# A new order by hand for the steady part of a fused attention and maxout kernel: 151 visits, searched on

## The chip, the cores and the metric

The kernel runs on one core of a Trainium2 chip. A core has a matrix engine (TensorE, PE in the profile), two engines that can read the matrix engine's result memory PSUM (ScalarE, ACT; VectorE, DVE), a general engine (GpSimd, POOL) and a queue processor (SyncE, SP) that mostly issues DMAs. PSUM has eight banks here, each 128 rows of 512 float32. The metric is device time in microseconds (us) of one execution; lower is better.

## The reference

Two parts follow each other. First an induced-set attention over x of shape (4, 12544, 128) with 32 inducing vectors, then a maxout layer over all 50,176 rows:

```python
def mab(q, kv):
    s = scale * (q @ kv.transpose(0, 2, 1))
    s = s - s.max(-1, keepdims=True)
    a = np.exp(s)
    a /= a.sum(-1, keepdims=True) + 1e-09
    return a @ kv
h = mab(I, x)          # 32 summary rows for each of the 4 batches
y = mab(x, h)          # each row of x attends to the 32 summary rows
h1 = y @ w1            # 128 -> 1024
h2 = y @ w2
out = np.maximum(h1, h2) @ w_out   # 1024 -> 128
```

## The kernel before

**The algebra.** max(h1, h2) is written as h1 + relu(h2 - h1). Since y is a mix of 32 rows of h, both parts are products of the 32 unnormalized exponentials of a row with small matrices made once per batch: `hwd` (32 x 1024, for h2 - h1) and `m1` (32 x 128, for h1 through w_out). Dividing by the sum of exponentials is left to the end, one factor per row.

**The tiling.** The 98 tiles of 128 rows in each batch are grouped in blocks. A block has four row groups q = 0 to 3, one for each quarter (32 rows) of the matrix engine's array, with up to four tiles in each; shapes are listed in `shapes`. There are 28 blocks, 0 to 27, seven to a batch, and 108 groups (a block's q with its tiles).

**The pieces of work in the steady part.** Each is a word of a list.

- `s` stages a block: scores of its tiles (L655) and their exponentials by ScalarE (L665).
- `p` is a visit: the array is used as four row quarters, and each pick names a quarter, a PSUM bank and who empties it. A pick makes one bank of h2 - h1 (L964). Then `relu_out` moves it to memory through a relu, on ScalarE (pick ends in `a`, L910) or VectorE (`v`, L908). A pick with `+` is emptied together with the next one as a double piece of 1024 columns. Endings `l`, `k`, `L` add the `m1` products of a group. Several `p` words without other work of TensorE between them make one visit; there are 151 visits.
- `d` with a count makes that many products of relu tiles with w_out (L843) into the open group's bank; `o` opens a group in a bank. When a group has all its products, `evict_group` multiplies it with the reciprocals and stores it: on VectorE (L878), or on ScalarE (L885) where the string `EVICT` has a 1; the store is a DMA on SP's queue (L893), from one of six buffers.
- The reciprocals of a block's sums come in one of two ways. `g` has SP transpose the exponentials by DMA (L699), and POOL adds them up and raises them to the power -1 (L708, L712). `n` makes the sums with TensorE (L727, four columns for each tile) and VectorE takes the reciprocal (L736); `n` with a plus does two blocks.
- `x`, `c`, `r`, `t`, `a`, `e`, `h`, `w`, `m` prepare the next batch: DMA transposes of x on SP (L230), scores and exponentials (L391, L403), DMA transposes of these on SP (L421), the accumulation of h (L436, L466/L468), and the small matrices (L475, L510, L561, L569).

**What sets the order.** `PLAN` is a list of such words, written out by hand from a search, and `play` issues their instructions in that order on every engine. Each engine and each queue runs its own instructions in order; semaphores hold an instruction until its data and its buffer are there. So the list fixes the order of TensorE's work, the order in which each evicting engine takes its banks, and the order of DMAs on SP's queue.

```python
if vector:
    nc.vector.tensor_scalar(out=dst, in0=src, scalar1=0.0, scalar2=None, op0=ALU.max)
else:
    nc.scalar.activation(out=dst, in_=src, func=AF.Relu)
...
for word in PLAN.split():
    play(word)
```

The first 22 us (loads, transposes and the first batch's summary) are issued ahead of the list and have an order of their own, `HEAD`.

Of the kernel before, what the change touches and what calls it, by code (L numbers as in the profile page):

```python
# [144 lines left out]
def kernel(  # L145
# [114 lines left out]
    with tc.manual_schedule(engines={ET.PE, ET.DVE, ET.Activation, ET.Pool, ET.SP}):  # L260
# [612 lines left out]
        def evict_group(g):  # L873
            osb = osbs[:, evicted[0] % NOUT, :, :]
            evicted[0] += 1
            q, n, blk = g.q, g.n, g.blk
            if EVICT[groups.index(g)] == "0":
                nc.vector.tensor_mul(  # L878
# [136 lines left out]
        p02a24a33vl:0000213 d17 p05v17a20a31v s2 g3 s3 o4 d17 p06+17a35vl p00+11a32v:021 d15 o3 d6 x1.6 x1.7  # L1015
        p07v15+26a32v d18 p04a17a20+31v p02a15+26al:0023100 d8 o4 d11 p17v20v31al d13 p12+33a p05+26v c1.0.7 s1
        d8 o0 d7 p02+13v25+36a x1.8 d9 p07v14a31a d13 p02v23a35vl p16a34a p07a d3 o1 d22 g4 p06a12+33vl p05v
        p14a c1.1.0 s7 d10 o6 d12 p04a12v23al p10v25v37a x1.9 d17 p04a11+22a33v x1.10 t1.1 g6 d3 o0 d21
        p17v25a34vl p01a12+23a36v:1203 d11 o5 d18 p07v21a34vl p26v p12a33a d12 p00+21a37v c1.2.2 c1.3.4 t1.3 g5
        d2 o3 d12 p00+11v26a37a d19 p02v15al p04v10+21a36a:3012 d1 o7 d19 p05a12v24al d13 o0 d12 p11a p03v26v32a  # L1020
        p17v24+35al:1023000 d20 o1 d9 p23v32al p06a27v p14a35v:10 d8 r1.0 d14 p06v12+23a37v c1.4.4 c1.5.0 a1.1.5
        a1.3.6 p32a t1.5 p03a17v d1 o5 d22 p04a16+37vl p00+11a22v33a d10 o4 d25 p06+17a20vl a1.5.1 p12a p03v25v
        d2 p00+11a26+37a d3 e1.2 d2 o3 d15 h1.5 d5 p10+21a32vl p06a14+25a37v:120310 d12 o2 d10 w1.0.0.0 d2 s1 s7
        s6 p05v10a23+34v d12 w1.1.1.1 d8 o6 d7 p27v35aLl p00a13a24a31v d9 o5 d18 s2 p10v37vl p01a16a23+34a d14
        o2 d7 m1.0 p06+27a31vl d9 o5 d10 p00v13v24vl p01+12a26a37a d18 x2.0 d4 o3 d7 p02a10+21a36a p04vl:100 g8
        x2.1 x2.2 d9 o7 d9 g9 d3 p15v p02a24a33a p00a11vl:2100 d4 o6 d16 n2 d5 p04+15a31a p17v23a32vl:2013000
        d11 o0 d10 x2.3 p27a34v p05a22v31al:0100023 d14 p23a p06v17v34a d8 o5 d6 p11+32a p06v23a x2.4 d20 x2.5
        p14a27v30v p01+12a36al:1203000 d6 o3 d14 p14a p07v x2.6 x2.7 p00+11a22vl:0000321 d10 p05+16v24a37a d7
        x2.8 x2.9 d1 o2 d14 p00a11v24v35a p16+27al d18 o3 d11 p05a10+21v34v p06a27a32al:1023000 d21
        p00a15+26v31v s7 c2.0.4 o2 d19 p03a30vl g10 p06+17a24v35a:1032 d13 o1 d11 x2.10 p03a p10v26v37a d7  # L1030
        p02a14+25vl c2.1.3 s0 c2.2.7 t2.1 g11 d14 o6 d11 p14a22+33vl p05a10a27v31a:1203 d21 p04+15a22+33v c2.3.0
        o7 d23 p21a p05+36vl p00v13+24a32a:2031 d9 o1 d20 p15a36vl p03v14a20a32a:0132 d12 o7 d10 p04v15+26a33v
        d18 p00v p11a g12 p22a p04+15a26vl:0000123 d4 o3 d18 p00+11v22a36v d10 r2.7 s4 c2.4.5 c2.5.2 a2.1.7
        p20+31v p14a25a36al:0100023 t2.3 d4 o7 d22 p02a14v20a31v p05+26a33al:1023000 t2.5 d10 o2 d19 p34v
        p00+11a p07a15a36vl:0000312 g13 d13 o3 d15 p00+11v24a p06al:00001 p17a p22a d17 o5 d5 p04v16a20+31a
        a2.3.7 a2.5.3 p02a14v26v37a d8 p13v20a31al d13 p24v p02a17a36a e2.0 d6 o3 d17 p01+12a24v37v
        p05+26a30al:1023000 d15 o4 d14 p11v32v p07a p05+16a33al:0000231 d15 h2.0 d3 o1 d10 p02v10a26+37v
        p05a13a24al:1012031201202 d12 w2.0.0.0 w2.1.2.1 d10 p05v13v26a37a s4 s0 s2 m2.1 o6 d21 p07v25a34a
        p13v21a30al:1023000 d11 o2 d8 o5 d5 p27a34vLl s3 p06v11+22a30v d14 p37v p04a13a26v d13 p02a10+21a34v o7
        d8 o6 d7 p03v22a35aL d12 p00+21a34v x3.0 p02+13a37vl:1023000 d13 o5 d15 p04a10+21vl g15 p02a16+27a33a  # L1040
        d17 o4 d12 p12v20al p31a p05a16v27a:120 d4 n3 d16 o0 d2 p06a11+22v33a x3.1 d21 p35a p06+27a34vl:0120003
        p01v12+23a:201 x3.2 g16 d9 o5 d16 x3.3 x3.4 p04v16a27a31v g17 x3.5 d16 o0 d5 p02a13v34aL
        p01v16+27al:1203000 d23 p02v13a24+35a d4 o1 d21 x3.6 p06v17a23a32v p14+25a30vl d11 o7 d20 p02+13a26v30v
# [61 lines left out]
```

## Time and profile before

| what | value |
| --- | --- |
| median of three runs | 311.86 us (311.69 to 312.07) |
| the profiled execution, its own time | 311.63 us |
| its span, first to last instruction | 309.9 us |
| mean granted TensorE clock | 0.999 of full speed |
| TensorE busy | 303.4 us |
| ScalarE, VectorE busy | 272.6 us, 271.8 us |
| POOL busy | 128.6 us |
| DMA | 55.55 MB, 179 GB/s on the mean |

Busy times are of the profiled execution and are shares of its span. A matrix product's row in the timeline has its start and a modelled end, and products are pipelined, so the distance between two starts says more than the length of one. "Idle before" in a group row is time in which the engine waited ahead of those instructions, and the arrow names what ended most of it.

### The profile page before, as it was taken

The numbers are of one execution on the slowest core, as the hardware profiler recorded it, in microseconds if no ns is written. First come the engines' busy times: TensorE is split into PE (matmuls) and PEld (weight loads), VectorE is DVE, ScalarE is ACT, GpSimd is POOL, SyncE is SP. The second block draws the span as 40 slices with busy tenths as digits, with TensorE's granted clock in tenths as the row PEclk, the third lists the DMA queues.
The fourth block names the chain that finished last, engine by engine and source line by source line (L and its number), as shares of the span: only waits on it lengthen the run. The fifth ranks groups of instructions, "written<-read, shape, count | busy, mean of one in ns | idle before, by whom it ended". The sixth has DMA issues, their size and how long they took to land.

```text
span 309.9 us, 12504 instructions
## 1 busy us (share of the span) xinstructions
PE 303.4 (98%) x5304; PEld 239.0 (77%) x5304; DVE 271.8 (88%) x443; ACT 272.6 (88%) x478; POOL 128.6 (42%) x194
## 2 busy tenths in 40 slices
PE   7899999999999999999999999999999999999996
PEld 3786777777878787778887887687878877788885
DVE  3369999999888999998899889998899899998995
ACT  3579999998899999899999999989899899988782
POOL 7473003466420084089700187019408916085200
PEclk9999999999999999999999999999999999999999
DMA  7999999995499999999699989994534323333223
GB/s 204 208 227 212 216 227 230 217 197 179 112 223 245 215 222 179 246 239 209 128 246 249 222 172 211 199 229 147 143 93 131 122 78 112 121 122 113 104 98 127
DMA packets 81528, 55.55 MB, mean 179 GB/s; under 512 B 62880, under 2 KB 66496, under 8 KB 81472
## 3 DMA queue, kind: packets, MB, share of 16 engines
q1 hardware_dynamic: 75168, 41.25, 57.1%
q0 software_dynamic: 6160, 13.44, 22.8%
q8 instruction: 41, 0.67, 0.9%
q14 instruction: 15, 0.12, 0.1%
q10 hardware_dynamic: 144, 0.07, 0.1%
HBM read 27.28 MB, written 25.69 MB: 171 GB/s over the span
## 4 chain that ended last, share of the span: by engine, by line
PE 93%; DMA 2%; DVE 2%; issue 1%; ACT 1%; POOL 1%; POOLq 0%; DVEq 0%
PE psall L843 61%; PE psall L964 23%; DMA xn<-in_x_dram 2%; PE psall L655 2%; PE psall L391 2%; PE psall L436 1%; PE psall L298 1%; DVE relus L908 1%; PE psall L360 1%; PE psall L314 1%; ACT xT L305 1%; PE psall L561 0%; POOL xn L222 0%; PE psall L475 0%; DVE osbs L878 0%
## 5 line engine op out<-in xcount | busy, mean ns | idle before, releaser
L910 ACT ACTIVATE relus<-psall 128x512 f16<-128x512 f32 (+1 forms) x371 | 233.7, 718 | 21.7 <-PE psall L964 20.4
L908 DVE TENSOR_SCALAR relus<-psall 128x512 f16<-128x512 f32 (+1 forms) x267 | 194.1, 770 | 18.6 <-PE psall L964 17.1
L843 PE MATMUL psall<-woutp,relus 128*128 128x128 f16 x3104 | 201.1, 219 | 0.0
L843 PEld LDWEIGHTS <-relus 128*128 128x128 f16 x3104 | 174.7, 98 | 31.2 <-issue 26.4
L964 PE MATMUL psall<-e,hwd 32*128 32x512 f16 (+2 forms) x840 | 80.0, 361 | 0.1
L708 POOL TENSOR_TENSOR half<-ed 128x256 f32<-128x256 f16 (+2 forms) x23 | 14.1, 615 | 139.1 <-DMA ed<-e 139.1
L712 POOL TENSOR_TENSOR rd<-den,minus 128x16 f32<-128x16 f32 (+2 forms) x23 | 60.7, 2641 | 1.8
L878 DVE TENSOR_TENSOR osbs<-psall,rd 128x512 f32<-128x512 f32 (+1 forms) x86 | 54.5, 636 | 2.1 <-PE psall L859 0.7
L964 PEld LDWEIGHTS <-hwd 32*128 32x128 f16 x880 | 27.3, 91 | 14.8 <-issue 2.2
L964 PE MATMUL psall<-m,e 32*128 32x128 f16 x376 | 36.6, 216 | 0.0
L964 PEld LDWEIGHTS <-e 32*128 32x128 f16 x376 | 22.5, 92 | 6.3 <-issue 0.5
L708 POOL TENSOR_TENSOR half<-half 128x64 f32<-128x64 f32 (+3 forms) x69 | 22.4, 325 | 5.4
L222 POOL DMA_DIRECT2D xn<-in_x_dram x34 | 18.7, 560 | 5.4 <-DMA xn<-in_x_dram 4.2
L878 DVE TENSOR_TENSOR osbs<-psall,rp 128x512 f32<-128x512 f32 (+3 forms) x20 | 12.8, 642 | 0.9 <-ACT relus L910 0.5
L302 DVE COPY xT<-psall 128x512 f16<-128x512 f16 (+3 forms) x12 | 5.8, 486 | 7.9 <-PE psall L298 7.2
L665 ACT ACTIVATE e<-psall 128x512 f16<-128x512 f32 (+2 forms) x21 | 11.2, 588 | 0.1
L403 ACT ACTIVATE eu<-psall 128x512 f16<-128x512 f32 x18 | 10.9, 610 | 0.0
L305 ACT COPY xT<-psall 128x768 f16<-128x768 f16 (+3 forms) x10 | 5.7, 577 | 4.3 <-PE psall L298 4.2
L298 PE MATMUL psall<-identity,xn 128*128 128x128 f16 x98 | 7.8, 220 | 1.3 <-DMA xn<-in_x_dram 1.1
L655 PE MATMUL psall<-xT,hT 128*32 128x512 f16 (+3 forms) x110 | 8.4, 360 | 0.0
L298 PEld LDWEIGHTS <-xn 128*128 128x128 f16 x98 | 5.6, 98 | 2.9 <-DVE xn L757 1.0
L391 PE MATMUL psall<-xT,inducingT 128*32 128x512 f16 x72 | 6.6, 385 | 0.0
(121 smaller groups left out, 124.5 us busy)
## 6 DMA issues: line engine op xcount, KB each, us to landing
out_dram<-osbs SPq DMA_DIRECT2D x90, 256.0 KB, 2.7
xn<-in_x_dram POOLq DMA_DIRECT2D x23, 448.0 KB, 10.9
out_dram<-osbs SPq DMA_DIRECT2D x10, 128.0 KB, 3.2
xn<-in_x_dram POOLq DMA_DIRECT2D x3, 224.0 KB, 8.9
xT<-xn SPq DMA_TRANSPOSE x33, 4.5
relus<-in_x_dram SPq DMA_DIRECT2D x1, 512.0 KB, 3.7
relus<-in_moe_w_dram POOLq DMA_DIRECT2D x2, 256.0 KB, 5.7
relus<-in_x_dram SPq DMA_DIRECT2D x1, 384.0 KB, 4.2
```

Source lines behind the costliest of these rows:

```text
L222: nc.gpsimd.dma_start(out=xn_at[b, i][p0:p1, 0:n, :], in_=xr[b, p0:p1, k0 : k0 + n, :])
L298: nc.tensor.transpose(ps[:, j, :], xn[:, g + j, :], identity16)
L391: nc.tensor.matmul(out=ps[32 * g : 32 * (g + 1), :], lhsT=inducingT, rhs=xT_tiles[b % 2][:, U * u + 4 * g : U * u + 4 * (g + 1), :], start ...
L655: nc.tensor.matmul(out=ps[32 * q : 32 * (q + 1), 128 * t : 128 * (t + n)], lhsT=hq, rhs=xT[:, c : c + n, :], start=True, stop=True, tile_p ...
L665: nc.scalar.activation(out=blk.e2[:, 0 : 128 * wd], in_=ps[:, 0 : 128 * wd], func=AF.Exp, scale=st[0]["rs"] if blk.b == 0 else scale,)
L708: nc.gpsimd.tensor_tensor(out=dst, in0=cur[:, :, 0:n], in1=cur[:, :, n : 2 * n], op=ALU.add)
L712: nc.gpsimd.tensor_tensor(out=rp[:, 0:wd, :].rearrange("p t q -> p (t q)"), in0=den[:, 0 : 4 * wd], in1=minus1[:, 0 : 4 * wd], op=ALU.pow,)
L843: nc.tensor.matmul(out=g.ps[:, 128 * t : 128 * (t + 1)], lhsT=home[:, 128 * (jb * w4 + t) : 128 * (jb * w4 + t + 1)], rhs=woutp[:, jb, :], ...
L878: nc.vector.tensor_mul(osb[:, 0:n, :], g.ps[:, 0 : n * C].rearrange("p (s c) -> p s c", s=n), blk.rp[:, 0:n, q : q + 1].broadcast_to((128, ...
L908: nc.vector.tensor_scalar(out=dst, in0=src, scalar1=0.0, scalar2=None, op0=ALU.max)
L910: nc.scalar.activation(out=dst, in_=src, func=AF.Relu)
L964: nc.tensor.matmul(**seq.pop(0))
```

## The change

The word list `PLAN` is replaced by another, and the string `EVICT` has no 1 any more. The new list was searched on from there while transfer times were drawn at random and ScalarE and VectorE were stopped at random moments. It plays the same kinds of words for the same blocks and groups with the same 151 visits. What differs is which bank and which engine a pick takes, how the picks of a visit are ordered and paired, where products are split, where the transposes on SP stand, and for which blocks the reciprocals are made by `n` instead of `g`: `n` now serves blocks 0, 1 and 2, 5 and 6, 7 and 8, and 14; before, 0, 1 and 2, 7, and 14. Nothing else in the kernel changes.

```diff
@@ -1008,65 +1008,64 @@
         PLAN = """
-        s6 s5 V0.0.0 H1.0.0 V1.7.1 p02+13v24a p06v10a:110000 p15a p11v27a:1010 W4.0 o0.1 d4.1 d4.1 p22v33a
-        p05a26a m0.7 o4 d4 n1 d8 p23v32aLl:23012122 p07v25a31a:021111 d4 o6 d10 x1.0 p13+24a32v p35a p37v
-        p01a30vl:00012 d14 x1.1 p04a12+23a37v o5 d14 x1.2 p06v10+21a34v d9 x1.3 p07a12v23al d9 p06v10a21a34a
-        x1.4 x1.5 o7 d16 n2+ d1 p03v p15a20a p16v21vl d13 p22a p14a p03v35a d2 o6 d15 p00a31v
...
-        x2.1 x2.2 d9 o7 d9 g9 d3 p15v p02a24a33a p00a11vl:2100 d4 o6 d16 n2 d5 p04+15a31a p17v23a32vl:2013000
...
-        d17 o4 d12 p12v20al p31a p05a16v27a:120 d4 n3 d16 o0 d2 p06a11+22v33a x3.1 d21 p35a p06+27a34vl:0120003
...
-        p06v10+21a37a:1203 o3 d22 p02v24+35a p10+21a36vl:1023000 d10 o7 d3 g25 d7 p02v14v25a36a d14 g27 p23a
...
-        o0 d19 p06+17a33v g26 p01+12a35vl:0000123 d13 o4 d15 p03a16v27al p05a10a21+32v d17 o3 d13 p05v16+27a31v
-        p12a20al d19 o5 d13 p04a16+27v31v p02+23a30al:10230100 d19 o4 d11 p26a p12+33v p17v20+31al:0021321 d5 o5
-        d17 p12+33a p06v10a31vl:010230023 d15 o7 d7 p06a23+34a p01+22v30vl:0012323 d9 o5 d22 p06a11a22vl
-        p07a10a23+34v:0312312 d10 o6 d16 o2 d7 p01a17a23+34v p00aLl:20101 d9 o5 d16 p01v17v23v34a p10a26al d16
-        o1 d24 o2 d16 o1 d8
-        EVICT = "000000000000000000000000000000000000000000000000000000000000000000000000000000000000000000000000000010010000"
+        s6 s5 V0.0.0 H1.0.0 V1.7.1 p02+13v p04v16a20a:21210000 p15a21a p17v W6.0 o0.1 d4.1 d4.1 p22v33a p05a24a
+        m0.1 o6 d4 n7 d8 p23v32aLl:23012122 p01a25v37a:021111 d4 o4 d10 p02+13a36v x1.0 p31a p35v p07a30vl:00012
+        d14 x1.1 p06a12+23a35v o1 d12 p00v16+27a34v d12 p05a12v23al d6 p06+27a x1.2 x1.3 p10a34v x1.4 d2 o5 d16
+        n2+ d1 p23v p14al p16+27v31a:210 d12 p12a p00a24a33v d3 o1 d14 p26a p07v32vl p00a33a d14 p06a14+25v37a
+        s0 s2 d4 o3 d17 p36v p04+15a p00+11a37vl:0000312 x1.5 g3 g4 d15 o2 d5 x1.6 x1.7 p06a14v25v37a d2 x1.8
...
+        p04a11+22vl d8 p03a15a26+37a e1.4 d4 o1 d16 h1.2 n3+ d4 p04+15a20v32v p13a26+37al d12 o0 d7 w1.0.4.0 d5
...
+        g9 p01vl:100 x2.0 d7 o0 d15 x2.1 x2.2 x2.3 x2.4 p05v13v21+32a p06a17al:1200 d1 o4 d13 g10 d3 n5+ d6
...
+        p00+11a36a p25a d16 o2 d13 p23+34v p00+31a p16+27al d3 n5 d16 p03a10+21v34a x3.5 o5 d23 p36a p02+13a27v
...
+        p14v26+37al:0000123 d12 o5 d10 p03v14a21+32a g26 d10 p20v p36a p07a23+34vl:0100023 d12 o1 d15
...
+        p02a15+26a34v:1230 d11 o0 d19 g25 p02+13a27v p34v p05+26a31vl:1023000 d13 o7 d22 p02+13a34v
...
+        p07v16a23+34v p01+22a30al:10230100 d16 o6 d16 p27v p11+32a p13a24v30aL:0021321 o5 d22 p06+17v31a
+        p02a13a34al:001230023 g27 d10 o0 d14 p21v32v p03a26+37al:0102323 d2 o5 d20 p04a11a23vl p02v10v26+37a d12
+        o4 d16 o3 d5 p01+22v30a p06a17aLl:3201013 d11 o5 d15 p06a12a20+31a p14v27al d17 o3 d24 o6 d16 o4 d8
+        EVICT = "000000000000000000000000000000000000000000000000000000000000000000000000000000000000000000000000000000000000"
```

More of the change, by code (lines that the diff above doesn't have):

```diff
@@ L1016 @@
[L1016 to L1025, printed above, removed]
@@ L1031 @@
[L1031 to L1040, printed above, removed]
@@ new lines @@
+        d17 p03a20+31v p14a p06+17a25al:1020300 d8 o3 d11 p14v20v31al d13 p02v16+27a34v s5 c1.0.1 d8 o0 d8
+        p02v14v26+37a d7 p25v p03a31al d16 p32v p04a16+27a33a p15v d1 o1 d21 p04a12vl p05+16v37a:201 s0 c1.1.3
+        d11 o4 d11 p02v p17a20a p05v16a23vl:0000123 x1.9 d17 p07a10v21+32a d4 o5 d20 p03v10v26+37a p11v22a34al
+        d12 o3 d18 p26a p07v20v32al:0130002 p11v34a d13 p05+26a37v c1.2.2 x1.10 c1.3.0 t1.1 t1.3 d1 o4 d11
+        p01a15+26v37a d20 p02v13a30vl p01a p15a26a d1 o7 d21 p03a12v21al d11 o0 d11 p25a34v p16al
@@ new lines @@
+        p03+14a27v30a d2 o6 d17 h3.5 p02+13a27v34v d12 w3.0.1.1 p00v15a37vl s2 s3 s4 d3 o1 d14 p10a25vl g22 g21
+        p07v16a22+33a d18 o4 d11 p00v15+26v37a p12+23a31al d21 o7 d4 w3.1.0.1 p05a12+23v36a:1203 d19
+        p01a14v20v35v p02a23a36al d9 o1 d21 p03+14a p02a30vl:020202021 p15v26a d11 o7 d5 p00v13+34al m3.5 d3 o2
+        d18 p00+11a26vl p04+15v27a33a d14 o6 d8 o0 d17 p04+15a21v37v p12+23aLl:1230111 d15 o1 d17 p04a15v27a36a
+        p02v23a30al:1023000 d15 o4 d15 p25v p06+37a p01+12a33vl:2013000 d17 o0 d3 p07a13a25+36v d20
```

56 lines of the change are left out of this document (32 added, 24 removed).

## The prediction

> **What bounds the kernel now.** I read the page from the top: busy shares, granted clock, then the chain that ended last. After these I took the timeline of TensorE alone, because a busy TensorE in this profile is not yet a TensorE without waits. The page:
>
> ```profile
> span 309.9 us, 12504 instructions
> PE 303.4 (98%) x5304; PEld 239.0 (77%) x5304; DVE 271.8 (88%) x443; ACT 272.6 (88%) x478; POOL 128.6 (42%) x194
> PEclk9999999999999999999999999999999999999999
> PE 93%; DMA 2%; DVE 2%; issue 1%; ACT 1%; POOL 1%; POOLq 0%; DVEq 0%
> PE psall L843 61%; PE psall L964 23%; DMA xn<-in_x_dram 2%; PE psall L655 2%; PE psall L391 2%; PE psall L436 1%; PE psall L298 1%; DVE relus L908 1%; PE psall L360 1%; PE psall L314 1%; ACT xT L305 1%; PE psall L561 0%; POOL xn L222 0%; PE psall L475 0%; DVE osbs L878 0%
> ```
>
> The reader is to see that TensorE holds 93% of the chain, 84 of it in two lines: the products with the output weights (L843) and the visits (L964). The clock is full throughout. The DMA share, 2%, is the first load, which the change does not touch.
>
> Now the prices of TensorE's two kinds of work, from the timeline of TensorE (start, length, line, count):
>
> ```profile
> 257.16 0.73 PE L843 MATMUL psall<-woutp,relus 128*128 128x128 f16 x10
> 257.82 0.40 PE L964 MATMUL psall<-e,hwd 32*128 32x512 f16 x4
> 258.15 1.51 PE L843 MATMUL psall<-woutp,relus 128*128 128x128 f16 x24
> 259.60 0.60 PE L964 MATMUL psall<-e,hwd 32*128 32x512 f16 x5
> ```
>
> Ten products last 0.73 us and 24 last 1.51: 0.78/14 = 0.056 us each. From the start of the 24 to the next visit are 1.45 us; less 24 x 0.056 that leaves 0.11 us for going into a visit. The visit at 257.82 has four matrix products of 512 columns side by side; the next product starts 0.33 us later. At 0.056 us for 128 columns, 512 columns take 0.22, so 0.11 us is the way out. A visit without a wait therefore costs its longest row group's columns, at 0.43 us per 1024, plus 0.11.
>
> With these I held each of the 151 visits against its start and the start of what followed. The first, the last and the two with the longest waits but one in the middle of the run:
>
> ```profile
> 23.64 1.31 PE L964 MATMUL psall<-e_first,hwd 32*128 32x128 f16 x20
> 24.93 0.61 PE L618 MATMUL psall<-woutp,relus 128*128 128x128 f16 x8
> 28.92 0.93 PE L964 MATMUL psall<-e_first,hwd 32*128 32x512 f16 x3
> 30.11 0.40 PE L843 MATMUL psall<-woutp,relus 128*128 128x128 f16 x4
> 281.88 0.39 PE L964 MATMUL psall<-e,hwd 32*128 32x512 f16 x3
> 282.65 1.74 PE L843 MATMUL psall<-woutp,relus 128*128 128x128 f16 x28
> 302.27 0.40 PE L964 MATMUL psall<-e,hwd 32*128 32x512 f16 x11
> 302.82 2.41 PE L843 MATMUL psall<-woutp,relus 128*128 128x128 f16 x40
> ```
>
> The first has 2048 columns in its fullest row group: 0.85 + 0.11 = 0.96 us, and it takes 1.29, so it waits 0.32. The visit at 28.92 (also 2048) takes 1.19 and waits 0.23. The one at 281.88 has 1024: 0.54 due, 0.77 taken, 0.23 of wait. The last takes 0.55 and waits hardly at all. Summed so over all 151, the visits wait **3.3 us**, and ten visits carry 1.8 of it. The product runs wait nowhere: each comes out at its count times 0.056 plus the 0.11, to within 0.04 us. So the list before is already within about 3 us of what its TensorE work costs. No list with the same work can gain more than that, while it may lose any amount.
>
> **The change part by part.** I walked both lists by the code and counted.
>
> *TensorE's own work.* Visits 151 and 151; columns of the fullest row group summed over visits 124,928 and 124,928; matrix products in visits 1,266 and 1,266; L843 products 3,136 and 3,136; stagings, scores, accumulations and the steps into and out of visits are the same in number. Result: 0. One thing is added. The reciprocal sums go through TensorE (`n`) for blocks 0, 1, 2, 5, 6, 7, 8, 14 instead of 0, 1, 2, 7, 14; blocks 5, 6, 8 have 4 + 2 + 4 = 10 tiles more. Their price and the evictions':
>
> ```profile
> 101.58 0.24 PE L727 MATMUL psall<-ones_q,e 128*128 128x4 f16 x4
> 101.68 0.44 PE L843 MATMUL psall<-woutp,relus 128*128 128x128 f16 x5
> L736 DVE RECIPROCAL rp<-psall 128x16 f32<-128x16 f32 (+1 forms) x4 | 1.1, 277 | 0.0
> L910 ACT ACTIVATE relus<-psall 128x512 f16<-128x512 f32 x276 | 148.9, 611 | 15.0 <-PE psall L964 14.0 <-ACT relus L910 0.4
> L910 ACT ACTIVATE relus<-psall 128x1024 f16<-128x1024 f32 x95 | 96.2, 1030 | 6.7 <-PE psall L964 6.4 <-ACT relus L910 0.2
> L908 DVE TENSOR_SCALAR relus<-psall 128x512 f16<-128x512 f32 x224 | 143.9, 683 | 13.3 <-PE psall L964 12.2 <-ACT eu L403 0.4
> L908 DVE TENSOR_SCALAR relus<-psall 128x1024 f16<-128x1024 f32 x43 | 52.5, 1220 | 5.3 <-PE psall L964 4.9 <-ACT relus L910 0.3
> L878 DVE TENSOR_TENSOR osbs<-psall,rd 128x256 f32<-128x256 f32 x7 | 2.9, 417 | 0.4 <-PE psall L859 0.4
> L885 ACT ACTIVATE osbs<-psall,rd 128x128 f32<-128x128 f32 x4 | 1.3, 382 | 0.0
> POOL half L708 <- DMA ed<-e: 139.1, 15, 25.5
> ```
>
> Four such tiles take 0.10 us until the next product starts: 10 x 0.026 = **+0.26 us**, on the path, since TensorE has no slack to hide it.
>
> *What that takes away.* Three of 23 DMA transposes of exponentials on SP's queue and three chains of adds and a power on POOL. POOL waited 139.1 us for such transposes, and SP waits for evictions, so this gains 0. The cover is that idle time.
>
> *ScalarE and VectorE.* Relu evictions go from 279 single and 95 double banks on ScalarE to 262 and 108, on VectorE from 229 and 43 to 228 and 39. By busy time per piece (0.539, 1.013, 0.642 and 1.221 us): ScalarE -17 x 0.539 + 13 x 1.013 = +4.0, less the four L885 pieces (1.3) that the new eviction string gives to VectorE: +2.7 us, to 275.3. VectorE -0.6 - 4.9 + 2 x 0.41 + 0.28 = -4.4 us, to 267.4. What lies on the path of this is only what makes a visit wait for a bank. From below that is -2.7 us: all waits of 3.3 but those of the first two shown, right behind the start-up, which stays as it is. From above it is 13 more double evictions, each 0.42 us longer in a bank than a single one: +5.5. The value taken is 0, and the row it is nearest to is this count: by the prices above, reuses of a bank with less than 1.0 us between its last write and its next (1.5 for a double eviction) number 81 in the old list and 81 in the new (single 51 to 55, double 30 to 26). Equal tightness, equal waits.
>
> *SP's and POOL's order.* The transposes of x and of the exponentials move between the stores by some microseconds; the tight one is block 25 (rivals). The x transposes of the last batch end later, at 201 against 196 us by the prices, and still lie 10 us ahead of the scores that read them. Taken: 0.
>
> *The tail.* The last visit gives ScalarE five banks and VectorE one, against three and three. The row at 302.82 has 40 products until the last groups, and ScalarE's last eviction would end some 0.4 us ahead of the products that read it. Taken: 0, with that little cover.
>
> Sum: the profiled execution took 311.63 us around its span of 309.9, so 311.63 + 0.26 = 311.9; the median, 311.86, lies 0.23 above that execution, so **312.1 us**, 0.1% more. The bound for no change, 0.2%, is 0.6 us here.
>
> **The rivals.**
>
> *A. Waits alike* (the forecast). For it: equal counts of tight reuses and equal TensorE work. Against it: 3.3 us of waits are the sum of a few accidents (ten visits carry 1.8), and another list has other accidents. I allow 0.8 either way, a quarter of the total: 311.3 to 312.9.
>
> *B. The new order takes waits away.* For it: VectorE is relieved by 4.4 us while ScalarE has no more than 275, tight double reuses fall from 30 to 26, and removable waits are 2.7. Against: single tight reuses rise. Half of the removable ones gone: 312.1 - 1.4 = 310.7; all gone: 309.4. The Trainium skill, page TensorEngine Tiling (Array Packing), section PSUM Bottleneck, says that tiling speeds up the matrix products and not the emptying of their banks, which can then be the limit; by that rule B's full gain, 309.4, would be the sum. The trace agrees only in part: both evictors are 88% busy and no product run waits.
>
> *C. More double evictions hold banks too long* (slower). It acts inside the visits, in the words with `+` ending in `a`. At the old rate, 3.3 us over 95 double evictions or 0.035 each, 13 more cost 0.45, which A's range holds. At a quarter of the upper bound they cost 1.4: 313.5. It decides once a double eviction delays a visit by 0.1 us on the mean. The Trainium skill, page Perfetto Trace Analysis, section Optimizing Scalar/DVE Operations, advises breaking instructions up when such engines are not saturated but cause bubbles elsewhere, so it speaks against this change; by it the sum would be C's 313.5. With both engines at 88% the trace shows neither case cleanly.
>
> *D. Block 25's reciprocals come late* (slower). Its transpose moves behind the store of block 24's first group. The rows:
>
> ```profile
> 271.87 0.67 POOL L708 TENSOR_TENSOR half<-ed 128x256 f32<-128x256 f16 x1 [9.04 <-DMA ed<-e]
> 274.17 2.91 POOL L712 TENSOR_TENSOR rd<-den,minus 128x16 f32<-128x16 f32 x1
> 278.99 0.68 DVE L878 TENSOR_TENSOR osbs<-psall,rd 128x512 f32<-128x512 f32 x1
> 279.70 3.55 SPq L893 DMA_DIRECT2D out_dram<-osbs  x2
> 283.35 1.19 SPq L699 DMA_TRANSPOSE ed<-e  x1
> 285.70 0.43 POOL L708 TENSOR_TENSOR half<-ed 128x128 f32<-128x128 f16 x1 [3.44 <-DMA ed<-e]
> 288.71 0.69 DVE L878 TENSOR_TENSOR osbs<-psall,rd 128x512 f32<-128x512 f32 x1
> DMA to landing us min/median/max: 2.3/3.6/7.4
> ```
>
> The store goes at 279.70, so the transpose at about 280.1; POOL starts 2.35 us after an issue (283.35 to 285.70) and needs 5.2 for a block four wide (271.87 to 277.08): ready at 287.7. VectorE needs it at 288.71. The cover is 1.0 us; a landing over 3.3 us decides it. VectorE takes its work in order, so relu evictions would stand behind. The longest landing, 7.4, would be 4 us late; I take 1.5 us on the path: 313.6.
>
> **How the numbers follow.** Chances: A 0.45, B 0.32, C 0.15, D 0.08. A's own range splits about 0.04 faster, 0.23 same, 0.18 slower; B is faster but for 0.01; C and D are slower. Faster 0.35, same 0.24, slower 0.41. The range 310.4 to 313.5 leaves out B's best part (about 0.1) and what of C and D goes beyond (0.1).
>
> **What would show it.** Right: L843 and L964 hold the same counts, L727 makes 30 instead of 20, product runs still step at 0.056, and visit waits sum to 2.5 to 4.1 us. B: the sum is under 2.5. C: long visits end with a ScalarE double eviction. D: VectorE's L878 at block 25 waits for POOL. What makes the prediction wrong most easily is a product run that waits for a relu eviction: the trace before shows none, so it does not show how near any of them is.

## The result, and the profile after

The changed kernel takes 314.10 us (median of six runs, 313.48 to 314.41) against 311.97 us for the kernel before, measured beside it (six runs). The ratio is 1.0062 with a 95% interval of 1.0048 to 1.0075: slower by 2.1 us by the medians, more than the 0.6 us that the prediction counts as no change. The profiled execution took 314.33 us around a span of 312.6.

The page of the changed kernel, the lines that answer to those of before:

```profile
span 312.6 us, 12488 instructions
PE 304.8 (98%) x5314; PEld 239.9 (77%) x5314; DVE 268.4 (86%) x441; ACT 275.2 (88%) x470; POOL 116.1 (37%) x176
PEclk9999999999999999999999999999999999999999
PE 89%; DMA 4%; DVE 3%; POOL 2%; issue 1%; ACT 0%; SPq 0%; DVEq 0%; POOLq 0%
PE psall L843 57%; PE psall L964 22%; DMA xn<-in_x_dram 2%; PE psall L655 2%; PE psall L436 1%; PE psall L391 1%; DMA ed<-e 1%; DVE relus L908 1%; PE psall L298 1%; POOL rd L712 1%; DVE osbs L878 1%; PE psall L360 1%; PE psall L314 1%; POOL half L708 1%; PE psall L561 0%
```

TensorE's share of the chain falls from 93% to 89%, and in its place stand three names that were not there: the landing of a transpose of exponentials (`ed<-e`, 1%), POOL's power on it (`rd` L712, 1%) and POOL's adds (`half` L708, 1%). The chain now runs through a block's reciprocals, and its part there is a stretch in which TensorE's order no longer sets the end. Busy TensorE grows by 1.4 us only, and the clock is full as before. ScalarE has 275.2 us, VectorE 268.4.

The groups of instructions with their shapes kept apart (count; busy time and mean ns of one; idle time ahead of them):

```profile
L910 ACT ACTIVATE relus<-psall 128x512 f16<-128x512 f32 x258 | 140.4, 607 | 13.2 <-PE psall L964 12.6
L910 ACT ACTIVATE relus<-psall 128x1024 f16<-128x1024 f32 x108 | 109.6, 1031 | 8.3 <-PE psall L964 7.7
L908 DVE TENSOR_SCALAR relus<-psall 128x512 f16<-128x512 f32 x224 | 144.1, 685 | 18.0 <-PE psall L964 17.3
L908 DVE TENSOR_SCALAR relus<-psall 128x1024 f16<-128x1024 f32 x39 | 47.5, 1220 | 3.6 <-PE psall L964 2.8 <-ACT e L665 0.7
L878 DVE TENSOR_TENSOR osbs<-psall,rd 128x512 f32<-128x512 f32 x65 | 44.4, 683 | 2.3 <-POOL rd L712 1.2 <-PE psall L843 0.4 <-PE psall L964 0.3
L727 PE MATMUL psall<-ones_q,e 128*128 128x4 f16 x26 | 1.2, 165 | 0.0
L727 PE MATMUL psall<-ones_q,e_first 128*128 128x4 f16 x4 | 0.2, 165 | 0.0
```

The sums through TensorE are 26 + 4 = 30, ten more than before, and the double evictions are 108 and 39, as counted. New is the 1.2 us for which VectorE's evictions of groups (L878) wait for POOL's `rd`.

To see where the 2.1 us lie I cut both profiled executions in three, at starts of TensorE's instructions, and summed the waits of the 151 visits as the prediction does:

| us | before | after | difference |
| --- | --- | --- | --- |
| span start to first visit | 23.64 | 24.18 | +0.54 |
| first visit to the start of the last product | 283.05 | 284.64 | +1.59 |
| start of the last product to the end | 3.18 | 3.73 | +0.55 |
| visit waits, within the middle part | 3.25 | 4.46 | +1.21 |

The first row is code that both kernels share, and in the nine profiled executions that have that code as it is it lies between 23.64 and 24.45 us, so I lay none of it to the change. The middle grows by 1.21 us of visit waits and by 0.25 us for the ten tiles (L727 from starts: 0.52 to 0.77 us); the other 0.13 us are the net of small differences, of which the scores of the next batch (L391, 0.28 us more) are the largest. The end grows by 0.55 us. A single visit carries nearly all of the new waits. Its rows in the timeline of the changed kernel (start, length, engine, line):

```profile
280.84 0.33 SPq L893 DMA_DIRECT2D out_dram<-osbs  x1
281.27 2.82 SPq L699 DMA_TRANSPOSE ed<-e  x1
285.73 0.67 POOL L708 TENSOR_TENSOR half<-ed 128x256 f32<-128x256 f16 x1 [9.48 <-DMA ed<-e]
288.03 2.91 POOL L712 TENSOR_TENSOR rd<-den,minus 128x16 f32<-128x16 f32 x1
290.20 0.50 PE L964 MATMUL psall<-e,hwd 32*128 32x256 f16 x7
290.98 0.69 DVE L878 TENSOR_TENSOR osbs<-psall,rd 128x512 f32<-128x512 f32 x1 [1.25 <-POOL rd L712]
291.72 0.39 PE L964 MATMUL psall<-e,hwd 32*128 32x512 f16 x2 [1.02 <-DVE osbs L878]
292.04 1.12 PE L843 MATMUL psall<-woutp,relus 128*128 128x128 f16 x17
```

The same visit and its transpose, read downwards: the store leaves SP, block 25's transpose goes out behind it at 281.27, POOL starts on its data only at 285.73, its power ends at 290.94, VectorE stands 1.25 us for it, and the visit begun at 290.20 cannot go on until VectorE has emptied a bank: 1.30 us of wait in all.

### The profile page after: what moved, and what is told of

Read it like the earlier page. It is cut to its first block, busy times and chain, and to the rows that moved or that the text cites. A ratio compares the mean times of both kernels' runs of the same rounds, so it can differ in the third digit from the quotient of the medians.

```text
span 312.6 us, 12488 instructions
## 1 busy us (share of the span) xinstructions
PE 304.8 (98%) x5314; PEld 239.9 (77%) x5314; DVE 268.4 (86%) x441; ACT 275.2 (88%) x470; POOL 116.1 (37%) x176
## 4 chain that ended last, share of the span: by engine, by line
PE 89%; DMA 4%; DVE 3%; POOL 2%; issue 1%; ACT 0%; SPq 0%; DVEq 0%; POOLq 0%
PE psall L843 57%; PE psall L964 22%; DMA xn<-in_x_dram 2%; PE psall L655 2%; PE psall L436 1%; PE psall L391 1%; DMA ed<-e 1%; DVE relus L908 1%; PE psall L298 1%; POOL rd L712 1%; DVE osbs L878 1%; PE psall L360 1%; PE psall L314 1%; POOL half L708 1%; PE psall L561 0%
## 5 line engine op out<-in xcount | busy, mean ns | idle before, releaser
L910 ACT ACTIVATE relus<-psall 128x512 f16<-128x512 f32 (+1 forms) x366 | 236.2, 732 | 21.4 <-PE psall L964 20.3
L908 DVE TENSOR_SCALAR relus<-psall 128x512 f16<-128x512 f32 (+1 forms) x263 | 189.9, 764 | 21.6 <-PE psall L964 20.1
L843 PE MATMUL psall<-woutp,relus 128*128 128x128 f16 x3104 | 201.2, 219 | 0.0
L843 PEld LDWEIGHTS <-relus 128*128 128x128 f16 x3104 | 174.7, 98 | 31.4 <-issue 26.2
L964 PE MATMUL psall<-e,hwd 32*128 32x512 f16 (+2 forms) x840 | 80.2, 361 | 1.1 <-DVE osbs L878 1.0
L708 POOL TENSOR_TENSOR half<-ed 128x256 f32<-128x256 f16 (+2 forms) x20 | 12.3, 617 | 151.1 <-DMA ed<-e 151.1
L712 POOL TENSOR_TENSOR rd<-den,minus 128x16 f32<-128x16 f32 (+2 forms) x20 | 53.3, 2663 | 1.6
L878 DVE TENSOR_TENSOR osbs<-psall,rd 128x512 f32<-128x512 f32 (+1 forms) x76 | 48.3, 638 | 3.8 <-PE psall L859 1.3
L964 PEld LDWEIGHTS <-hwd 32*128 32x128 f16 x880 | 27.8, 91 | 16.6 <-issue 3.6
L964 PE MATMUL psall<-m,e 32*128 32x128 f16 x376 | 37.1, 216 | 0.0
L964 PEld LDWEIGHTS <-e 32*128 32x128 f16 x376 | 22.7, 92 | 5.7 <-issue 0.8
L708 POOL TENSOR_TENSOR half<-half 128x32 f32<-128x32 f32 (+4 forms) x60 | 19.6, 326 | 4.7
L878 DVE TENSOR_TENSOR osbs<-psall,rp 128x512 f32<-128x512 f32 (+3 forms) x32 | 20.0, 625 | 1.2 <-PE psall L964 1.0
```

What stands on the lines that cost most here:

```text
L708: nc.gpsimd.tensor_tensor(out=dst, in0=cur[:, :, 0:n], in1=cur[:, :, n : 2 * n], op=ALU.add)
L712: nc.gpsimd.tensor_tensor(out=rp[:, 0:wd, :].rearrange("p t q -> p (t q)"), in0=den[:, 0 : 4 * wd], in1=minus1[:, 0 : 4 * wd], op=ALU.pow,)
L843: nc.tensor.matmul(out=g.ps[:, 128 * t : 128 * (t + 1)], lhsT=home[:, 128 * (jb * w4 + t) : 128 * (jb * w4 + t + 1)], rhs=woutp[:, jb, :], ...
L878: nc.vector.tensor_mul(osb[:, 0:n, :], g.ps[:, 0 : n * C].rearrange("p (s c) -> p s c", s=n), blk.rp[:, 0:n, q : q + 1].broadcast_to((128, ...
L964: nc.tensor.matmul(**seq.pop(0))
```

## The experiments

In the edits, a list word stands as in the diff. "Landing" is the time from the issue of a DMA transpose on SP to its last packet in the trace's packet records; POOL waits for the semaphore that a DMA sets when it is done, and its row starts 0.5 to 0.7 us after that last packet in the cases shown here. "Before" beside a result is the kernel before, run on the same chip. Three chips were used, on which the kernel before has medians of 311.91 us (experiments 1 to 4), 312.06 (5 to 7) and 311.68 (8 and 9), so tenths of a microsecond between experiments of different chips mean little.

**1. Block 25's transpose earlier, alone.** In the changed list the word `g25` goes from behind `o0 d19` to behind `g26`:

```diff
-        p14v26+37al:0000123 d12 o5 d10 p03v14a21+32a g26 d10 p20v p36a ...
+        p14v26+37al:0000123 d12 o5 d10 p03v14a21+32a g26 g25 d10 p20v p36a ...
...
-        p02a15+26a34v:1230 d11 o0 d19 g25 p02+13a27v p34v ...
+        p02a15+26a34v:1230 d11 o0 d19 p02+13a27v p34v ...
```

> The changed list with one word moved: the DMA transpose of block 25's exponentials stands right behind block 26's, some 10 us earlier on SP's queue. Theory L (block 25's reciprocals land late and hold VectorE, and this is most of the loss): the 1.3 us wait of the visit at 290 us is gone, the time falls from 314.1 to about 312.8, ratio to before about 1.003. Rival theory S (the loss is spread over many visits or lies in the tail, and the wait at 290 us would be made up elsewhere): 313.8 to 314.2, ratio 1.006.

The transpose is then the second of the two that SP issues from 270.15 on, some 10 us earlier.

Measured: 313.05 us (11 runs; before 311.91), ratio 1.0033 [1.0024, 1.0042]. The visit in question in its timeline:

```profile
289.37 0.68 DVE L878 TENSOR_TENSOR osbs<-psall,rd 128x512 f32<-128x512 f32 x1
289.93 0.50 PE L964 MATMUL psall<-e,hwd 32*128 32x256 f16 x7
290.48 1.96 PE L843 MATMUL psall<-woutp,relus 128*128 128x128 f16 x32
```

VectorE's eviction no longer waits, the visit takes 0.55 us from start to start, and the visit waits of the whole list sum to 3.15 us, against 3.25 in the kernel before. The middle part is 283.33 us: 1.31 less than in the changed kernel, which is the wait, and 0.28 more than before, about the price of the ten tiles. The end is still 3.74 us. So the place of one word on SP's queue costs 314.10 - 313.05 = 1.05 us by the medians, and the rest of the 2.1 us is elsewhere.

**2. The same word late, in the old list.**

```diff
-        ... d10 o7 d3 g25 d7 p02v14v25a36a d14 g27 p23a
+        ... d10 o7 d3 d7 p02v14v25a36a d14 g27 p23a
...
-        ... p13v21+32al:0000123 d8 o4 d21 p00a13a26+37v ...
+        ... p13v21+32al:0000123 d8 o4 d21 g25 p00a13a26+37v ...
```

> The kernel before with one word moved: the transpose of block 25's exponentials stands behind the store of block 24's first group, as in the changed list. Theory L with the cover as I worked it out (1.0 us): if landing takes 2.35 us as elsewhere in this stage, nothing changes, 311.9; if the place itself makes the landing slow, up to 1.3 us more, 313.2. Theory F (the 4.5 us to landing in the changed kernel come from a 16 KB instruction fetch on one of the DMA engines at the same moment): it depends on where the fetch falls here; in the profile of before it falls at 281.6, while this transpose would be issued at 280.1, so about 1 us more. Theory S: 311.9.

Measured: 312.82 us (before 311.91), ratio 1.0031 [1.0014, 1.0048]. The visit at 290.91 in its timeline waits 0.70 us, again for VectorE's eviction:

```profile
290.91 0.50 PE L964 MATMUL psall<-e,hwd 32*128 32x256 f16 x7
291.83 0.39 PE L964 MATMUL psall<-e,hwd 32*128 32x512 f16 x2 [0.42 <-DVE osbs L878]
```

0.70 us is smaller than the 1.30 of the changed kernel; here the transpose landed in 3.40 us instead of 3.87. The profiled execution has another wait, 0.99 us at 81.6 for a transpose of the next batch's exponentials, which is in no other profiled execution and which I leave out. The old list gets the same wait from the same word, so the wait belongs to the word's place, not to the new list's evictions.

**3. The old sums in the new list.** Blocks 5, 6 and 8 go back to the transposes; the ten tiles are gone.

```diff
-        ... t1.1 t1.3 d1 ...
+        ... t1.1 t1.3 g6 g5 d1 ...
...
-        ... d16 h1.2 n3+ d4 p04+15a20v32v ...
+        ... d16 h1.2 d4 p04+15a20v32v ...
...
-        g9 p01vl:100 x2.0 ... g10 d3 n5+ d6
+        g8 g9 p01vl:100 x2.0 ... g10 d3 n5 d6
```

> The changed list with the reciprocals of blocks 5, 6 and 8 made by DMA transpose and POOL again, as before the change. The term of 0.26 us for ten more tiles on TensorE: the time falls by 0.2 to 0.3 us, to 313.8. If the three transposes and stalls behind them cost more than that, it does not fall, 314.1 or more.

Measured: 313.46 us (before 311.91), ratio 1.0056 [1.0029, 1.0084]. The median is 0.64 us below the changed kernel's, but the intervals overlap, so a gain isn't shown. In its list of waits a line appears that the changed kernel does not have: TensorE's scores of the next batch wait for a transpose of x.

```profile
PE psall L391 <- DMA xT<-xn: 0.9, 1, 0.9
```

The 0.25 us of the ten tiles are saved, and the starts of L391 lose 1.3 us more than in the changed kernel. So the tiles' price stands, but it may have bought something. The transpose of x in question is issued 1.2 us later than in the changed kernel (118.98 against 117.80) and lands 1.35 us more slowly (5.12 us against 3.77 by its semaphore), with an instruction fetch at 121.83 in it; 4 and 5 are about such fetches. Yet in experiment 6, whose list lacks the three transposes, it is issued at 118.78 and lands in 5.12 us as well. So that the three transposes make the scores wait is not shown. As TensorE comes later here, the visit behind block 25 waits only 0.53 us, and the end, with the three transposes back, is 3.11 us; see 6. The experiment is therefore no clean price of the tiles.

**4 and 5. Why did the transpose land so late?** The packet records of the trace show, among the transposes' small packets, now and then one packet of 16 KB on a queue of its own. The page of the changed kernel names the queue, and a second one for instructions (packets, MB, share of 16 engines):

```profile
q8 instruction: 41, 0.67, 0.9%
q14 instruction: 15, 0.12, 0.1%
```

The 41 packets of 16 KB on q8 are 671,744 bytes, one about every 7 us; over TensorE's 2 x 5,314 matrix products and weight loads that is 63 bytes for each, which is why I take q8 for TensorE's instruction stream. The Trainium skill, page Runtime: NRT & Kernel Launch, section Instruction fetch mechanics, says that an engine's instructions are fetched in blocks of 16 KiB by a DMA queue of their own, and that the cost is mostly hidden. The trace agrees with the size of the block. As to hidden, I set the landings of transposes of block size in the last part of the run beside the fetches that fell into them:

| kernel, block | issue | landing | fetch within it, start (length) |
| --- | --- | --- | --- |
| before, 24 | 255.06 | 1.96 | none |
| before, 26 (two wide) | 283.35 | 1.66 | none |
| after, 25 | 281.27 | 3.87 | 281.79 (1.89) |
| after, 27 | 295.85 | 3.55 | 297.02 |
| experiment 1, 24 | 257.18 | 3.0 | 258.43 |
| experiment 2, 25 | 281.78 | 3.40 | 283.41 (0.95) |
| experiment 3, 25 | 281.47 | 3.60 | 283.11 (1.15) |

Without a fetch a full block lands in about 1.95 us, with one in 3.0 to 3.9.

The table is a selection; the whole set says the same. Over the eleven profiled executions, 44 transposes of exponentials issued after 215 us have no fetch between issue and landing; they land, by the semaphore, in 2.28 to 2.49 us. The 31 with a fetch that starts more than 0.25 us ahead of the landing take 2.88 to 4.59 us, and four with a fetch that starts later than that are not delayed.

To test this by hand and not by coincidence, the fetch had to be moved while the list stayed. The warm-up products at the start of the kernel, whose results nobody reads, do that: their number sets where in TensorE's stream the 16 KB borders lie. Both variants keep all or most of the warm-up's columns but use more instructions, 102 and 90 more with the weight loads, which should move the borders by an estimated 2.9 and 2.5 us at one border every 7 us.

Variant 4, nine products of 512 columns become four of 512 and 56 of 32:

```diff
-        for _ in range(WARM):
+        for _ in range(4):
             nc.tensor.matmul(...)
+        for _ in range(56):
+            nc.tensor.matmul(out=ps[:, 0:32], lhsT=warm[:, 0:128], rhs=warm[:, 0:32], start=True, stop=True)
```

> The changed kernel with the nine wide warm-up products ahead of the data replaced by four wide and 56 narrow ones, which TensorE does while it waits for the first load: 102 more TensorE instructions ahead of everything, so each 16 KB instruction fetch falls about 2.9 us earlier against the work. The list itself is untouched. Theory F: the transpose of block 25 lands in about 2.4 us instead of 4.4, the wait at 290 us shrinks from 1.3 to about 0.2 or less, the time falls to about 313.0. If the fetch has nothing to do with it: the same landing of 4.4 us and 314.1.

Variant 5, narrow ones first, 48 of 32 columns and then six of 512:

```diff
-        for _ in range(WARM):
+        for _ in range(48):
+            nc.tensor.matmul(out=ps[:, 0:32], lhsT=warm[:, 0:128], rhs=warm[:, 0:32], start=True, stop=True)
+        for _ in range(6):
             nc.tensor.matmul(...)
```

> The changed kernel, its list untouched (block 25's transpose late), with three of the nine wide warm-up products replaced by 48 narrow ones that stand first, so that the wide ones keep TensorE busy up to the first data: 90 more TensorE instructions, each 16 KB instruction fetch about 2.5 us earlier against the work. Theory F: block 25's transpose lands about 2 us after its issue instead of 3.9, the wait at 290 us is 0.2 us or less instead of 1.3, and, with the start as before, the time falls from 314.1 to 313.0. If only the place on SP's queue counts: 1.3 us of wait and 314.1. If the start is slowed again, the wait alone decides between the theories.

Measured, variant 4: 315.34 us (before 311.91), ratio 1.0100 [1.0069, 1.0131]; variant 5: 314.75 (before 312.06), ratio 1.0071 [1.0044, 1.0098]. Both expected 313.0, and as times they do not help. In variant 4 the first visit starts 25.70 us into the span, against 24.18, and the granted clock falls around it. TensorE by stretches of 2 us (stretch, length, busy time and count, granted clock, DMA share, GB/s):

```profile
20.00:22.00 2.00, 1.30 (x36) 1.00 1.36 168
22.00:24.00 2.00, 1.88 (x22) 0.84 1.34 209
24.00:26.00 2.00, 2.00 (x18) 0.50 1.05 205
26.00:28.00 2.00, 1.84 (x29) 0.80 1.09 217
28.00:30.00 2.00, 2.00 (x36) 1.00 1.05 208
```

The changed kernel has 1.00 in all of these. The dip comes 18 us behind the warm-up, so how the one leads to the other, if it does, is open. In variant 5 eight of the twelve runs have a mean granted clock of 0.983 to 0.995; the four at 0.999 or 1.0 took 312.71 to 314.03 us. A fetch also ran there from 306.16 to 307.62, into the last stores, and the end took 4.14 us. What the two were made for is in their traces. Variant 5, same list, same word, the timeline around block 25 (two lines further down in the code):

```profile
280.87 0.33 SPq L895 DMA_DIRECT2D out_dram<-osbs  x1
281.30 1.22 SPq L699 DMA_TRANSPOSE ed<-e  x1
283.77 0.67 POOL L708 TENSOR_TENSOR half<-ed 128x256 f32<-128x256 f16 x1 [6.05 <-DMA ed<-e]
286.06 2.91 POOL L712 TENSOR_TENSOR rd<-den,minus 128x16 f32<-128x16 f32 x1
290.23 0.50 PE L966 MATMUL psall<-e,hwd 32*128 32x256 f16 x7
290.78 1.96 PE L845 MATMUL psall<-woutp,relus 128*128 128x128 f16 x32
```

The transpose is issued at 281.30, as in the changed kernel to 0.03 us, behind the same store, and no fetch lies in it: the one that was at 281.79 is now at 278.18. It lands in 1.95 us, POOL starts 2.47 us after the issue instead of 4.46, and the visit waits for nothing. Variant 4 has 1.96 us and no wait either, and block 27's transpose, 3.55 us after the change, has 1.96 in both. So it is shown that the late landing goes when the borders of TensorE's stream are moved, with the word where it was.

How the 16 KB packet does it can be inferred from the packets. In the changed kernel the fetch lasts from 281.79 to 283.68. Of the transpose's 512 packets 479 have started by 283.33. From then to 284.6 all that starts, apart from one packet of 4 bytes, is eight packets of 2 KB of the stores beside it, one after the other, and only then, from 284.68 to 285.14, come the transpose's last 33. The late landings of experiments 1, 2 and 3 and of block 27 also have 33 or 34 packets that trail. These are about a sixteenth, and there are 16 DMA engines, so it looks as if the engine that carries the fetch does its share of the store and of the transpose late. The records do not name the engine of a packet, so this last step is not shown.

**6, 7. The end.** The end is 3.18 us before and 3.73 after, though the last packet of the stores ends 1.82 us after the last product starts before and 1.83 us after. (The very last group's store is issued on ScalarE's queue, all others on SP's.) What is longer is the closing steps on SP behind it: semaphore steps and drains under the kernel's last line. The rows of that line (count; duration ns; first and last start), first before, then after, then experiment 1:

```profile
L1100 SPq EVENT_SEMAPHORE  x11: 17/28/28, 307.3 to 309.8; - x11
L1100 SPq DRAIN  x3: 7/7/7, 309.0 to 309.3; - x3
```

```profile
L1099 SPq EVENT_SEMAPHORE  x11: 17/28/28, 309.5 to 312.5; - x11
L1099 SPq DRAIN  x3: 7/7/129, 311.3 to 312.0; - x3
```

```profile
L1099 SPq EVENT_SEMAPHORE  x11: 17/28/28, 307.9 to 310.9; - x11
```

The eleven steps, with the same median duration of one, stretch over 2.5 us before and 3.0 after and in experiment 1. The changed kernel has three transposes fewer on SP's queue (339 records on SP against 346), so I supposed that it matters where SP's own instruction stream ends. To test it, experiment 1's kernel gets three stores split in two DMAs, or eight, which changes nothing else in the kernel:

```diff
+            cuts = [(0, 2), (2, n)] if evicted[0] in (81, 84, 87) else [(0, n)]
+            for lo, hi in cuts:
+                queue.dma_start(out=outr[blk.b, :, c + lo : c + hi, :], in_=osb[:, lo:hi, :])
```

> The list of the run with block 25's transpose moved up, and three output stores of 256 KB (groups 81, 84 and 87) issued as two DMAs each, so SP's queue has about as many instructions as before the change. Theory T (the 0.56 us by which the end is longer comes from where SP's last instructions lie in its instruction stream, which is shorter by three transposes): the end, from the last matrix product to the last instruction, changes from 3.74 to about 3.15 us and the time from 313.05 to about 312.5. If the end hangs on the last stores themselves: 3.74 as before and 313.05. In between if three are too few.

> The same with eight stores (groups 81 to 88) issued as two DMAs each. Theory T: the end differs from the run with three, as the last instructions lie elsewhere again: either 3.1 to 3.2 us or 3.7, nothing in between, and the time follows, 312.5 or 313.05. If the end hangs on the last stores: 3.74 and 313.05 in both.

Measured: with three 311.89 us (12 runs; before 312.06), ratio 0.9986 [0.9968, 1.0004]; with eight 312.44 (12 runs), ratio 1.0000 [0.9981, 1.0019]. The closing rows with three split stores:

```profile
L1101 SPq EVENT_SEMAPHORE  x11: 17/28/28, 308.4 to 310.8; - x11
L1101 SPq DRAIN  x3: 7/7/7, 310.0 to 310.3; - x3
```

The steps stretch over 2.4 us again and the longest drain is 7 ns instead of 129; the end is 3.11 us. With eight it is 3.41, between the two values, which a mere "ahead of a border or behind it" does not give.

SP's records one by one show two causes instead of one. Times are from the start of the last product:

| kernel | DMAs on SP | last one's semaphore, checked in step | step passes | from there to first drain | first drain to end | 8 KB packet on q14 |
| --- | --- | --- | --- | --- | --- | --- |
| before | 175 | 117, eighth | 1.96 | 0.36 | 0.85 | 1.77 |
| after | 172 | 114, fifth | 2.00 | 0.49 | 1.24 | 3.47 |
| experiment 1 | 172 | 114, fifth | 2.00 | 0.49 | 1.25 | 3.48 |
| 6, three split | 175 | 117, eighth | 2.00 | 0.28 | 0.84 | 2.22 |
| 7, eight split | 180 | 114, fifth | 2.05 | 0.51 | 0.85 | 1.71 |

First, eight semaphores serve SP's DMAs in turn, and the closing steps check them in a fixed order. The number of DMAs thus decides how many checks still stand behind the one that waits for SP's last store. Three fewer transposes moved that check from the eighth step to the fifth, three split stores move it back, and eight, a full turn, leave it; this is worth 0.13 us between before and after, and 0.23 between 6 and 7. Second, the drains take 0.84 to 0.85 us or 1.24 to 1.25, and nothing between, in all eleven profiled executions. The long value goes with a packet of 8 KB on the second instruction queue, q14, that comes 3.5 to 3.9 us after the last product starts instead of 1.7 to 2.2. This fits theory T for that part, but whose instructions these are, and how they hold the drains, no trace here shows.

The gain of three split stores, 313.05 - 311.89 = 1.16 us, is also larger than the 0.63 us that the end explains. The other 0.5 is in no part of the profiled executions, and experiment 6's is the slowest of its twelve (312.67 us; the others took 311.77 to 312.12), so its trace does not show the usual run. So: that the end depends on what else SP issues is shown, and where it grows; why the drains are longer, and where the other 0.5 us comes from, is open.

**8. The split stores alone.** The changed list as it is, with the same three stores split.

> The changed kernel with block 25's transpose late as it is, and only the three stores split. If the two losses add up, the one at the end goes alone: 314.1 less 1.16 (what splitting gave with the transpose early) is 312.9, with the wait at 290 us still 1.0 to 1.3 us. If the split moved something else, such as the meeting of the transpose and the instruction fetch, the wait at 290 us is gone too: 311.9.

Measured: 312.81 us (before 311.68), ratio 1.0035 [1.0023, 1.0048]. The end is 3.12 us. The visit behind block 25 still waits, 0.63 us instead of 1.30. Its transpose is issued at 280.46, 0.8 us earlier in an execution whose first visit starts 0.5 us earlier, and lands in 3.33 us instead of 3.87, with a fetch at 282.02:

```profile
289.61 0.50 PE L966 MATMUL psall<-e,hwd 32*128 32x256 f16 x7
290.45 0.39 PE L966 MATMUL psall<-e,hwd 32*128 32x512 f16 x2 [0.35 <-DVE osbs L878]
```

With both edits nothing of the loss shows any more: the ratio is 1.0062 with both causes, 1.0033 without the late transpose, 1.0035 with the split stores, and 0.9986 with both edits, an interval that holds 1. One by one the edits gain 0.0029 and 0.0027, together 0.0076; whether the 0.0020 between them are more than the intervals' width of 0.001 to 0.002 on either side is open.

**9. One more wait taken away, wrongly.** In experiment 6's kernel a visit at 94.9 waits 0.37 us; I gave its picks other banks to spare that.

```diff
-        ... p01v26a37al d4 m1.4 d6 ...
+        ... p01v23a34al d4 m1.6 d6 ...
```

> The list of the run with block 25's transpose early and three stores split, and one more change: the visit that waited 0.37 us at 94.9 us for banks 6 and 7, both held by one double eviction of VectorE that had itself been late, takes banks 3 and 4 instead, and the small product behind it takes bank 6. If a wait inside a visit is time lost, as I priced it, 0.25 to 0.37 us go: 311.55 to 311.65 against 311.89, ratio to before 0.998 to 0.999. If the wait comes back at the next reuse, 311.9.

Measured: 312.55 us (before 311.68), ratio 1.0022 [1.0006, 1.0039]. The same visit in the timeline of TensorE, first in experiment 6's kernel, then here:

```profile
94.87 0.66 PE L966 MATMUL psall<-e,hwd 32*128 32x512 f16 x3
95.36 0.28 PE L966 MATMUL psall<-e,hwd 32*128 32x256 f16 x2
95.57 0.40 PE L843 MATMUL psall<-woutp,relus 128*128 128x128 f16 x4
```

```profile
95.09 0.39 PE L966 MATMUL psall<-e,hwd 32*128 32x512 f16 x1
96.06 0.28 PE L966 MATMUL psall<-e,hwd 32*128 32x256 f16 x2 [0.58 <-DVE osbs L878]
96.39 0.28 PE L843 MATMUL psall<-woutp,relus 128*128 128x128 f16 x2
```

The new bank was held by VectorE's eviction of a group, so the wait is 0.97 us. The mistake serves as a measurement: 0.60 us more wait in one visit, and the median went from 311.89 to 312.55 us, 0.66 more, on another chip. With the 1.31 us by which the middle part shrank in experiment 1, this says that in this kernel a wait inside a visit goes into the time about whole.

No version here is shown to beat the kernel before; the one with the early word and three split stores ties with it.

## Why the prediction was wrong

The forecast was 312.1 us with a range to 313.5; the time was 314.10, which lies outside. By its own steps:

*The price of a visit.* The prediction works out 0.22 us for 512 columns, from 0.056 for 128, and then charges 0.43 for 1024, not 0.45. The visits bear the second: of the 62 with 512 columns none takes less than 0.32 us, of the 87 with 1024 none less than 0.53. As both lists have the same columns, the difference between them does not hang on it.

*TensorE's own work, 0.* Right. L843 has 3,104 rows in its large group in both, at 201.1 and 201.2 us busy; L964 has 840 and 376 in both.

*Ten more `n` tiles, +0.26 us.* Right: 0.25 us between starts.

*What that takes away, 0.* Right for POOL, which waits 151.1 us for such transposes now. For the scores of the next batch, which wait for x in experiment 3, it is open. For the end it was not nothing: with the three transposes back, experiment 3's end is 3.11 us instead of 3.73.

*ScalarE and VectorE, 0 on the path.* Right. ScalarE came to 275.2 us (forecast 275.3), VectorE to 268.4 (267.4; 0.8 of the difference lies in the single relu evictions, of which both traces hold 224 rows where the count has one fewer). With block 25's word early, in experiment 1, the visits wait 3.15 us against 3.25. Thirteen more double evictions cost nothing that shows. The equal counts of tight reuses, 81 and 81, thus go with equal sums, though one pair of lists does not show that the one makes the other. Rival A's mechanism holds for all visits but one, and rivals B and C fall. With C falls what the Trainium skill, page Perfetto Trace Analysis, section Optimizing Scalar/DVE Operations, would have advised for this case. Of the rule in the Trainium skill, page TensorEngine Tiling (Array Packing), section PSUM Bottleneck, that the emptying of banks can become the limit, nothing is seen beyond these 3 us: both evictors are 86 to 88% busy and the visits' waits are 1% of the span.

*SP's and POOL's order, 0.* **This step failed first.** Rival D named the place, the store ahead of block 25's transpose, the wait of VectorE's L878 for POOL, and a landing beyond 3.3 us as the point from which it decides; it got a chance of 0.08. The order of issue and POOL's 5.2 us came out as worked out. What failed is the 2.35 us from issue to POOL's start. It came from one row, block 26, two wide, whose transpose had no fetch in it. Here it was 4.46. The row quoted beside it, with landings of 2.3, 3.6 in the median and 7.4 at the most, already said that more than half of such landings exceed the limit of 3.3, but the sum did not use the median. In this stage the risk was smaller than that row: of the eight transposes that the kernel before issues after 215 us, seven land in 2.28 to 2.49 us and one, block 27's at 270.70, in 4.28, with a fetch at 272.47. So a late landing was in the trace, about one in eight, and that it fell on the one transpose with 1 us of cover was in part bad luck, while the term that let it count, a single landing time without its spread, was the error. Its price, taken as 1.5 us, is 1.05.

*The tail, 0, with 0.4 us of cover.* **This step failed too**, by +0.55 us in the trace, but not at the place where I looked. ScalarE's last eviction did not run out of cover; the last data lands as early as before. The closing steps on SP take longer, 0.39 us of it in the drains, and splitting three stores takes that away. The prediction had no term for what comes after the last store, though it counted three DMAs fewer on SP's queue; that the drains have two lengths shows only when several traces stand side by side.

*The sum.* Late transpose 1.05, end 0.55 in the trace and 1.16 by the medians of experiments 1 and 6, ten tiles 0.25: 1.85 to 2.46, against 2.13 measured. The terms come from different chips and executions, so the agreement is a rough one. The signs that the text named came out as follows: L727 makes 30, the runs of products step as before, L878 at block 25 waits for POOL, and the visit waits are 4.46 us, above the 2.5 to 4.1 of the forecast by the one visit. The text took a product run that waits for a relu eviction for the likeliest way to be wrong; that did not come.

## What to carry to other kernels

When a list of work is reordered on an engine that has no slack, look last at the engines that have plenty: one word placed 10 us later on SP's queue cost four times what the one counted change of TensorE's work did. Where a DMA has a cover of 1 us, hold that cover against the spread of its landings in the same stage of the trace, longest included, and not against the one landing that stands nearest; and see whether instruction packets lie in the late ones. And split a difference of two runs into start, middle and end before explaining it: 0.5 us of this one lay behind the start of the last product.

## What was not expected of the hardware

- Among the DMA traffic is an instruction stream, to all appearances TensorE's, 16 KB every 7 us or so. A DMA transpose of a full block that has such a packet in it lands in 3.0 to 3.9 us instead of 1.95, about a sixteenth of its packets trailing, and moving the stream by 90 or 102 instructions brings the 1.95 back. So the number of instructions in the warm-up has a say in which transpose, 280 us later, comes late.
- The closing steps on SP stretch over 2.4 to 3.0 us. They depend on how many DMAs SP issued, by the order in which eight semaphores are checked, and on drains that take 0.85 or 1.24 us, so three more stores on SP make the program end sooner.
- With 56 warm-up products of 32 columns in place of five of 512 the granted clock fell to 0.50 between 24 and 26 us, long after the warm-up, and the first visit came 1.5 us later. With 48 narrow ones first and six wide ones behind, the profiled execution has no such dip and its first visit at 24.21 us, though eight of its twelve runs had a mean clock of 0.983 to 0.995. The kernel before has 0.994 or 0.995 too, but in 4 of 27 and 6 of 29 runs. Changing a warm-up is thus, by these runs, not a neutral way to shift the instruction stream; why is open.
- The start, with the same code, took 23.6 to 24.5 us from one profiled execution to the next. Nothing in the traces says why.
